# Filler matmuls, earlier zero stores and an early start of two w2 passes in a decode step with its gradients

## The chip, the core and the metric

The kernel runs on one core of one Trainium2 chip. The metric is device time in microseconds (us), median of several runs. "Span" is the time from the first to the last instruction of one profiled execution; all positions such as "at 341.5" are us from the start of that span. Engines: TensorE (PE; PEld are its weight loads), VectorE (DVE), ScalarE (ACT), GpSimd (POOL), SyncE (SP). SP and POOL issue nearly all transfers (DMA).

## What is computed

One token passes through two layers of type A (attention over a cache) and two of type B (a Mish MLP), in the order A, B, A, B, with the same weights for both A and for both B; then the gradients of everything are computed.

```python
def A(x, k_cache, v_cache, wq, wo):     # x: 1 x 1024, 32 heads of 128, 4 KV groups
    W = 4096                            # the last 4096 of 32768 cached positions
    q = x @ wq                          # wq: 1024 x 4096
    p = softmax(q k^T / sqrt(128));  o = p v
    return o @ wo                       # wo: 4096 x 1024
def B(x, w1, b1, w2):
    h = x @ w1 + b1                     # w1: 1024 x 3584
    return (h * tanh(softplus(h))) @ w2 # w2: 3584 x 1024
x = x + A(layernorm(x)); x = x + B(layernorm(x))
x = x + A(layernorm(x)); x = x + B(layernorm(x))
# outputs: x, and the gradients of x, k_cache, v_cache, wq, wo, w1, b1, w2 for a given grad_out
```

All arrays are bf16. The gradients of the two caches are 33.5 MB each and zero outside the last 4096 positions: the zeros have to be written all the same.

## The kernel before

**Stages.** The layers are called A1, B2, A3, B4 by their order. The program's order is: `attn_fwd` A1; `mlp_fwd` B2, which also reads w2 for the part of its backward that needs only the known last gradient; `attn_fwd` A3; `mlp_turn` B4, forward through w1 and backward through it in blocks of 512 columns; `attn_bwd` A3; the w2 pass of B4 (`w2_pass`); `mlp_bwd_w1` of B2; `attn_bwd` A1; at last the dW stage, which makes all weight gradients and the cache gradients as outer products, evicts them and stores them. Vectors are held as columns, 128 to a column; a matrix times a vector is a row of products of 128 x 128 blocks with the weight block as the stationary operand and the vector broadcast to 16 columns (`mv`, through `mm` at L222), or, where the rows are summed in four column groups of TensorE, with the vector stationary and 512 columns moving (`row_mm`).

**Order.** The schedule is manual: each engine executes its instructions in the order in which the Python code records them, and waits for others by semaphores. What stands ahead on an engine's queue is therefore done first. Weight tiles come through the pool `strm` of 6 buffers (NB): a load on SP waits until its buffer is free, and all that SP has behind it waits too. Transposes go to a PSUM pool of 4 buffers (`psum1`) and are evicted by ScalarE or VectorE (`evac`, L145 and L148). The work pool has one buffer for each tag; `scr`, `yr`, `rep8`, `de`, `db_row` and others share the tag "kp".

**Zeros.** 112 stores of a 0.5 MB tile of zeros `zt` fill the unused part of the cache gradients. `bg_zeros(n, after)` (L138) issues n of them on POOL once `after` is there; `zeros(n)` (L129) issues n on SP. The dictionary `Z` says how many at which place: A3d are issued within `attn_bwd` A3 after the wo loop, A1c at the start of `attn_bwd` A1 on POOL, A1d there after the wo loop, on SP. What is left over by then, 5 stores, is issued one at a time between groups of nine dW jobs (`zeros(1)`, L1145).

**attn_bwd.** wo has 16 tiles, nine of which are kept in SBUF; the last seven ("late") are read again. The gradient is broadcast to all partitions (`bcast_row`, tile `gbc`: a VectorE copy `rep8` L580 and 8 matmuls). Then come products with kept tiles (`bwd_rows2`), 32 row matmuls into `drow`, and a loop over the late tiles: T(i) transposes half a tile, has ScalarE evict it and VectorE multiply and sum the other half with `gbc` (L781); M(i) multiplies the transposed half and, between tiles, does pieces of other preparation (`fill` in A3, `nextprep` in A1). After it: dO to a row and back (`dps`, `qps`), `rows_mm` with V (tile `d`), the softmax gradient, `cols_mm` with K, 64 row matmuls with wq (`nrow`), their copy `yr` (`rows_copy`, L238), a selection (`rows_sel2`), and the gradient of the norm (`ln_bwd`). The last work of `prep` in A1 is `db1_out`, the small bias gradient with its POOL store, and `rows_put` of dq for the dW stage.

**w2 pass.** For each of 14 tiles: forward products, 8 transposes (L602), eviction by ScalarE (L603), a VectorE reduction with `gbc` (L605), and, one tile later, the backward products.

**dW stage.** Each chunk is four matmuls into PSUM, evictions by both engines into a staging slot of 0.5 MB, and a store on SP.

Of the kernel before, what the change touches and what calls it, by code (L numbers as in the profile page):

```python
# [8 lines left out]
FP32 = mybir.dt.float32  # L9
BF16 = mybir.dt.bfloat16  # L10
# [4 lines left out]
P = 128  # L15
# [8 lines left out]
def kernel(  # L24
# [117 lines left out]
    def evac(out_ap, in_ap, cd, ca, how=None):  # L142
# [3 lines left out]
        else:  # L146
            ev[1] += ca
            nc.scalar.copy(out_ap, in_ap)  # L148

    def shaped(t, shape):  # L150
        n = 1
        for k in shape[1:]:
            n *= k
        ap = t[0:shape[0], 0:n]
        if len(shape) == 3:
            return ap.rearrange("p (a b) -> p a b", a=shape[1])
        if len(shape) == 4:
            return ap.rearrange("p (a b c) -> p a b c", a=shape[1], b=shape[2])
        return ap
# [110 lines left out]
    def ln_fwd(x_col, name):  # L270
# [3 lines left out]
        sps = sm_tile(P, 2 * TD)  # L274
        nc.tensor.matmul(sps[:], lhsT=onesD[:], rhs=xx[:], start=True, stop=True)
        s12 = work.tile([P, 2], FP32, name="s12")
        nc.vector.reduce_sum(s12[:], sps[:].rearrange("p (a b) -> p a b", a=2), axis=AX.X)
# [13 lines left out]
    def ln_bwd(dn_ps, n32, rstd, g_col, name, nxt):  # L291
# [4 lines left out]
        sps = sm_tile(P, 2 * TD)  # L296
        nc.tensor.matmul(sps[:], lhsT=onesD[:], rhs=tt[:], start=True, stop=True)
        ab = work.tile([P, 2], FP32, name="ab")
        nc.vector.reduce_sum(ab[:], sps[:].rearrange("p (a b) -> p a b", a=2), axis=AX.X)
# [286 lines left out]

    def w2_pass(a_bf, g_bf, x_col, xname, wgname, gbc, zn):

        acc = wide(TD + NW2)
        wg = keep.tile([P, NW2, 2], FP32, name=wgname)  # L590
        held = []

        def bwd1(w, c):
            for dch in range(TD):
                mv(acc, TD + c, w[:, 1, dch * P:(dch + 1) * P], g_bf[:, dch:dch + 1], False, dch == TD - 1)

        for c in range(NW2):
            w = pre.pop(0) if pre else w2_load(c)
            fwd_rows2(acc, w, c, a_bf, c == 0, c == NW2 - 1)
            ps = psum1([P, 8, P], BF16, "tps")  # L600
            for b in range(TD):
                nc.tensor.transpose(ps[:, b, :], w[:, 1, b * P:(b + 1) * P], ident_bf[:])  # L602
            nc.scalar.copy(w[:, 1, :], ps[:].rearrange("p b c -> p (b c)"))  # L603
            scr = work.tile([P, D], BF16, name="scr", tag="kp")
            nc.vector.tensor_tensor_reduce(out=scr[:], in0=w[:, 0, :], in1=gbc[:], scale=1.0, scalar=0.0,  # L605
                                           op0=ALU.mult, op1=ALU.add, accum_out=wg[:, c, 0:1])
            if held:
                bwd1(held.pop(), c - 1)
            if c == NW2 - 2 and zn:
                bg_zeros(zn, wg[:, c, :])  # L610
            held.append(w)
        bwd1(held.pop(), NW2 - 1)
        x_new = keep.tile([P, TD], FP32, name=xname)
        nc.vector.tensor_add(x_new[:], x_col[:], acc.cols(0, TD))
        nc.vector.tensor_copy(wg[:, :, 1:2], acc.cols(TD, TD + NW2)[:, :, None])
        return x_new, wg

    def mlp_fwd(x_col, lname, g_bf):

        n32, n_bf, rstd = ln_fwd(x_col, lname)  # L620
        sv = dict(n32=n32, rstd=rstd)
        hacc = wide(TF)
        h_init(hacc.t, 0, TF)
        for i in range(2 * TD):
            t, hf = i // 2, i % 2
            w = w1_load(i)
            for b in range(NW2):
                fb = hf * NW2 + b
                o = (b // 2) * 2 * P + b % 2
                mv(hacc, fb, w[:, o:o + 2 * P - 1:2], n_bf[:, t:t + 1], False, t == TD - 1)  # L630
        a_bf = pair_col("a", lname, TF)
        dact = keep.tile([P, TF], FP32, name=f"dact_{lname}")
        gbc = bcast_row(g_bf)
        m = mish_exp(hacc.cols(0, TF), TF)
        mish_w(m, hacc.cols(0, TF))
        nc.vector.tensor_mul(a_bf, m["hr"], m["w_"])
        mish_y(m)
        nc.vector.tensor_mul(dact[:], m["y"], m["r"])
        sv["dact"] = dact
        x_new, wg = w2_pass(a_bf, g_bf, x_col, f"x_{lname}", "wg4", gbc, Z["B2"])  # L640
        return x_new, sv, wg
# [103 lines left out]
    def attn_bwd(g_col, g_bf, lname, sv, first, nxt):  # L745
# [9 lines left out]
        drow = sm_tile(P, 512)  # L755
        wdo = work.tile([P, NO - NR], FP32, name="wdo")
        bwd_rows2(dacc, wo_kept[NR - 1], NR - 1, g_bf, started=False)
        for dch in range(TD):
            for q in range(4):
                row_mm(drow, q, g_bf[:, dch:dch + 1], wo_rows[:, 4 * q:4 * q + 4, dch * P:(dch + 1) * P], dch == 0, dch == TD - 1)  # L760
# [13 lines left out]

        def T(i):
            c = late[i]
            if c not in held:
                held[c] = wo_load(c)
            w = held[c]
            xpose(*nat_blocks(w[:, 1, :]), "a")  # L780
            nc.vector.tensor_tensor_reduce(out=w[:, 0, :], in0=w[:, 0, :], in1=gbc[:], scale=1.0, scalar=0.0,  # L781
                                           op0=ALU.mult, op1=ALU.add, accum_out=wdo[:, i:i + 1])

        def M(i, _):
            c = late[i]
            w = held.pop(c)
            for dch in range(TD):
                mv(dacc, 2 * c + 1, w[:, 1, dch * P:(dch + 1) * P], g_bf[:, dch:dch + 1], False, dch == TD - 1)
            if i == 0:
                for j in range(4):  # L790
                    mm(dacc.cols(j, 16)[:, 0:13:4], de[:, j * P:(j + 1) * P], ident_bf[:, 0:P:32], False, True)
            if first and i in (1, 3, 5):
                fill(1, ["V", "K", "wq"], "a")
            if not first and i:
                nextprep()

        pipe(list(range(len(late))), T, M)
        if first:
# [12 lines left out]
        if first:  # L811
            fill(1, ["K", "wq"], "a")
        dps = psum1([HQ, P], BF16, "dps")
        nc.tensor.transpose(dps[:, 0:P], do_p[:].rearrange("p t c -> p (t c)"), ident_bf[:])
# [4 lines left out]
        if first:  # L819
            fill(1, ["K", "wq"], "a")  # L820
        qps = psum1([P, NO, 2], FP32, "qps")
        for e in range(2):
            mm(qps[:, :, e], drf[:, e * P:(e + 1) * P], fold16[:], e == 0, e == 1)
        sv["dorep"] = pad_cols(pad, qps[:].rearrange("p c e -> p (c e)"), 1.0, f"do_{lname}")
        top("halves")
# [4 lines left out]
        else:  # L830
# [9 lines left out]
            ])  # L840
            nextprep(2)
        scr = work.tile([P, WC], BF16, name="scr", tag="kp")
        sdp = work.tile([P, 2], FP32, name="sdp")
# [16 lines left out]
        if first:  # L860
            fill(100, ["K"], "a")
        else:
            nextprep(1)
        for hf in range(2):
            half_T(ds, dsT, hf, "va"[hf])
# [6 lines left out]
        if first:  # L872
            fill(100, ["wq"], "av")
        else:
            prep.append(lambda: rows_put(area["Rq"], 1, "dq", "heads"))
        nrow = acc_tile(512)
# [6 lines left out]
        nps = sm_tile(P, TD)  # L883
        rows_sel2(rows_copy(nrow, "v"), Cols8(nps, True))
        return ln_bwd(nps[:], sv["n32"], sv["rstd"], g_col, lname, nxt)


# [152 lines left out]
    def after_do():  # L1040
        s0, s1, tall["w2"], area["do3"], area["q3"], _, r1 = cut_up(wo_flat, 0, (1024, 1024, 2560, 512, 512, 512, 2048))
        area["spread"] = [s.rearrange("p (j x) -> p j x", x=P) for s in (s0, s1)]
# [20 lines left out]

    Z = dict(B2=3, A3=16, B4=[5, 2, 1, 2, 1, 2, 6], A3c=6, A3d=29, W1=3, A1c=6, A1d=25)

# [41 lines left out]
    x3, sA3 = attn_fwd(x2, "A3", False)  # L1107
    g3, g3b, sB4 = mlp_turn(x3, "B4", wg4, gcol, "A3")
    g2, g2b = attn_bwd(g3, g3b, "A3", sA3, True, "B2")
    x4, wg2 = w2_pass(sB4["a_bf"], g2b, x3, "x_B4", "wg2", bcast_row(g2b), 0)  # L1110
    dh_of(wg2, "B2", sB2)
# [4 lines left out]
    def db1_out():  # L1116
        db1 = work.tile([P, 2, NW2], BF16, name="db1")
        nc.vector.tensor_add(db1[:], sB4["dh"][:].rearrange("p (c t) -> p t c", t=2), sB2["dh"][:].rearrange("p (c t) -> p t c", t=2))
        db_row = work.tile([NW2, P, 2], BF16, name="db_row", tag="kp", padded_shape=[NW2, WC // 2, 2])
        for t in range(2):  # L1120
            dbps = psum1([NW2, P], BF16, "dbps")
            nc.tensor.transpose(dbps[:], db1[:, t, :], ident_bf[:])
            nc.vector.tensor_copy(db_row[:, :, t], dbps[:])
        nc.gpsimd.dma_start(out_7.rearrange("(c x) -> c x", x=2 * P), db_row[:].rearrange("c p t -> c (p t)"))

# [53 lines left out]
```

## Time and profile before

| | |
|---|---|
| Time, median of 8 runs | 458.13 us (455.94 to 461.3) |
| Profiled execution, its own time | 459.46 us |
| Its span | 457.5 us |
| Moved by DMA | 172.23 MB, of it 98.58 MB written to HBM |
| Busy: PE / DVE / ACT / POOL | 71% / 52% / 49% / 13% of the span |
| Zero stores: on POOL / on SP | 82 / 30 |
| Mean granted TensorE clock | 0.739 |
| Last eviction of the dW stage ends | about 435.6 us |

The page cuts the span in 40 slices of 11.44 us; a digit gives the busy share of an engine in tenths, and the last row the transfer rate. An answer by stretches gives the same for chosen windows: busy us and number of instructions in brackets for PE, PEld, DVE, ACT and POOL, then the granted clock of TensorE as a share, the busy share of the DMA engines and GB/s. The chain of waits lists, in order of time, the start, the length and what the end of the program was waiting for at that moment; "DMA w_c<-in_B_w_dram" is the time from issue to landing of a load. The stages by their places in this execution: `attn_bwd` A3 from about 191 to 246, the w2 pass of B4 to 269, `mlp_bwd_w1` to 298, `attn_bwd` A1 to 348, dW from then on.

### The profile page before, as it was taken

To read this page: it belongs to the slowest core of one execution; us is meant where nothing else is said; L and a number is where in the kernel's file an instruction comes from. 1 tells how busy PE (TensorE), PEld (TensorE's weight loads), DVE (VectorE), ACT (ScalarE), POOL (GpSimd) and SP (SyncE) were. 2 spreads that over 40 slices of the span, in tenths; PEclk is the share of its full clock that TensorE was granted. 3 is DMA by queue.
4 is the path that set the end of the run, shared out by engine and by line. 5 is a ranking of instruction groups with operands and counts; after the bars stand their busy time and mean duration, and the time that the engine had idled before them with its cause. 6 is when DMAs were issued, how large, how long until landed. Compare 5 with 4: busy or idle time off the path is not lost.

```text
span 457.5 us, 11888 instructions
## 1 busy us (share of the span) xinstructions
PE 324.2 (71%) x5080; PEld 221.1 (48%) x5080; DVE 236.7 (52%) x489; ACT 225.0 (49%) x262; POOL 59.8 (13%) x152
## 2 busy tenths in 40 slices
PE   0465755586897989868897887776856858888700
PEld 0243534485567979845885877753522111112100
DVE  3124101385423757653265853572326978999900
ACT  1122100165332858774582653435214988999900
POOL 2000000002422112421331020062010000000000
PEclk9999555577977989995798788979675555556555
DMA  8999999989999998999999998999993999999997
GB/s 315 388 413 422 408 408 356 405 285 342 417 415 374 404 338 288 404 410 418 415 414 388 323 360 315 341 385 401 415 368 121 406 415 401 415 414 407 420 415 307
DMA packets 52256, 172.23 MB, mean 376 GB/s; under 512 B 5200, under 2 KB 12396, under 8 KB 51180
## 3 DMA queue, kind: packets, MB, share of 16 engines
q1 hardware_dynamic: 40256, 128.47, 72.6%
q0 software_dynamic: 11904, 43.01, 23.4%
q8 instruction: 39, 0.64, 0.5%
q14 instruction: 13, 0.11, 0.1%
q10 hardware_dynamic: 44, 0.01, 0.0%
HBM read 72.89 MB, written 98.58 MB: 375 GB/s over the span
## 4 chain that ended last, share of the span: by engine, by line
PE 23%; ACT 13%; DMA 9%; issue 4%; DVE 3%; DVEq 0%; POOL 0%; ACTq 0%; SPq 0%; POOLq 0%
PE tps L186 7%; ACT wq_b L148 6%; PE ops L222 5%; DMA w_c<-in_B_w_dram 4%; PE acc L222 4%; DMA out_dram<-st_o 2%; PE sm L222 2%; ACT wo_b L148 2%; DMA wo_c<-in_A_wo_dram 2%; ACT st_o L148 2%; PE d L222 2%; PE tps L602 1%; ACT wo_c L148 1%; ACT V L148 1%; DMA out_dram<-db_row 1%
## 5 line engine op out<-in xcount | busy, mean ns | idle before, releaser
L138 POOL DMA_DIRECT2D out_dram<-zt x82 | 43.6, 535 | 46.3 <-DMA out_dram<-zt 43.5
L222 PEld LDWEIGHTS <-w_c 128*128 128x128 bf16 x1120 | 35.8, 101 | 20.8 <-DMA w_c<-in_B_w_dram 13.4
L603 ACT COPY w_c<-tps 128x1024 bf16<-128x1024 bf16 x28 | 28.3, 1012 | 24.0 <-PE tps L602 12.5
L222 PE MATMUL ops<-V 2*128 2x512 bf16 (+1 forms) x160 | 33.5, 579 | 6.5 <-ACT wq_b L148 3.5
L605 DVE CUSTOM_DVE_ANT_0 scr<-w_c,gbc 128x1024 bf16<-128x1024 bf16 x28 | 34.2, 1221 | 6.8 <-DMA w_c<-in_B_w_dram 4.9
L145 DVE CAST wq_b<-ops 128x1024 bf16<-128x1024 f32 (+1 forms) x31 | 33.8, 1147 | 3.8 <-PE ops L222 3.3
L148 ACT CAST wq_b<-ops 128x1024 bf16<-128x1024 f32 (+1 forms) x33 | 33.7, 1140 | 2.2 <-PE ops L222 2.0
L148 ACT COPY K<-tps 128x1024 bf16<-128x1024 bf16 x19 | 18.7, 1024 | 29.3 <-PE tps L186 29.3
L222 PE MATMUL ops<-wo_b 2*128 2x512 bf16 x120 | 23.3, 567 | 10.9 <-ACT wq_b L148 7.2
L222 PEld LDWEIGHTS <-V 128*128 128x128 bf16 (+2 forms) x416 | 14.0, 101 | 27.6 <-issue 27.3
L222 PE MATMUL q<-wq_b,nA_pair 128*32 128x512 bf16 x128 | 12.6, 473 | 16.7 <-DMA wq_b<-in_A_wq_dram 15.2
L781 DVE CUSTOM_DVE_ANT_0 wo_c<-wo_c,gbc 128x1024 bf16<-128x1024 bf16 x14 | 16.4, 1219 | 12.5 <-DMA wo_c<-in_A_wo_dram 5.3
L148 ACT COPY w_b<-tps 128x1024 bf16<-128x1024 bf16 x20 | 19.5, 1015 | 5.3 <-PE tps L186 4.9
L145 DVE COPY K<-tps 128x1024 bf16<-128x1024 bf16 x13 | 8.8, 689 | 24.9 <-DMA wq_b<-in_A_wq_dram 14.1
L602 PE MATMUL tps<-ident_bf,w_c 128*128 128x128 bf16 x224 | 21.5, 254 | 0.0
L186 PE MATMUL tps<-ident_bf,w_c 128*128 128x128 bf16 x224 | 17.7, 241 | 4.2 <-DMA w_c<-in_B_w_dram 4.2
L222 PEld LDWEIGHTS <-wo_b 2*128 2x128 bf16 (+1 forms) x152 | 5.7, 100 | 29.3 <-issue 28.7
L186 PE MATMUL tps<-ident_bf,K 128*128 128x128 bf16 x256 | 19.6, 234 | 0.1
L148 ACT COPY w_c<-tps 128x768 bf16<-128x768 bf16 (+1 forms) x14 | 11.6, 829 | 15.9 <-PE tps L186 15.9
L222 PE MATMUL acc<-a_pair,w_c 128*128 128x16 bf16 x448 | 15.8, 172 | 4.7 <-DMA w_c<-in_B_w_dram 3.7
L145 DVE COPY w_c<-tps 128x1024 bf16<-128x1024 bf16 (+1 forms) x18 | 11.7, 660 | 13.6 <-PE tps L186 9.6
L148 ACT CAST K<-ops 128x1024 bf16<-128x1024 f32 x18 | 17.5, 1014 | 2.5 <-PE ops L222 1.9
(321 smaller groups left out, 665.5 us busy)
## 6 DMA issues: line engine op xcount, KB each, us to landing
out_dram<-zt POOLq DMA_DIRECT2D x82, 512.0 KB, 10.4
out_dram<-zt SPq DMA_DIRECT2D x30, 512.0 KB, 7.9
wo_c<-in_A_wo_dram SPq DMA_DIRECT2D x28, 512.0 KB, 8.0
w_c<-in_B_w_dram SPq DMA_DIRECT2D x32, 448.0 KB, 6.3
w_c<-in_B_w_dram SPq DMA_DIRECT2D x28, 512.0 KB, 6.5
out_dram<-wq_b SPq DMA_DIRECT2D x17, 512.0 KB, 9.9
wq_b<-in_A_wq_dram SPq DMA_DIRECT2D x16, 512.0 KB, 10.8
out_dram<-K SPq DMA_DIRECT2D x8, 1024.0 KB, 8.6
```

The lines of the kernel that those rows point to most:

```text
L138: nc.gpsimd.dma_start(zero_jobs.pop(0), zt[:])
L145: nc.vector.tensor_copy(out_ap, in_ap)
L148: nc.scalar.copy(out_ap, in_ap)
L186: nc.tensor.transpose(ps[:, b, :], ap, ident_bf[:])
L222: nc.tensor.matmul(out_ap, lhsT=lhsT, rhs=rhs, start=start, stop=stop, skip_group_check=True, **kw)
L602: nc.tensor.transpose(ps[:, b, :], w[:, 1, b * P:(b + 1) * P], ident_bf[:])
L603: nc.scalar.copy(w[:, 1, :], ps[:].rearrange("p b c -> p (b c)"))
L605: nc.vector.tensor_tensor_reduce(out=scr[:], in0=w[:, 0, :], in1=gbc[:], scale=1.0, scalar=0.0, op0=ALU.mult, op1=ALU.add, accum_out=wg[:, ...
L781: nc.vector.tensor_tensor_reduce(out=w[:, 0, :], in0=w[:, 0, :], in1=gbc[:], scale=1.0, scalar=0.0, op0=ALU.mult, op1=ALU.add, accum_out=w ...
```

## The change

A function `warm(n)` is new: n matmuls of the identity with itself, 512 columns wide, into a PSUM tile that nobody reads. It is called with 6 in the norm of A3 forward, with 7 in the norm's gradient ahead of `attn_bwd` A1, and with 4, 2, 2, 3 and 3 within `attn_bwd` A1: 27 matmuls.

In `attn_bwd` T(0), T(1) and M(0) are issued before the row matmuls `drow`; the products with `de` move from M(0) to M(1).

The w2 pass becomes a class whose steps can be called apart. In B2 the broadcast is recorded ahead of the w1 loop, the transposes of tile 0 ahead of the second part of the Mish activation, and `mish_y` and `dact` after the last tile. In B4 tile 0 is transposed while `yr` is copied in `attn_bwd` A3 ("copy"), its forward products and eviction follow the selection ("sel"), and those of tiles 1 and 2 follow the norm gradient's sum ("ln").

`rows_put` of dq leaves the list `prep` and stands behind the copy of `yr`. `db_row` lies in a part of the kept wo area that was unused, not in a tile of tag "kp".

Zeros: A3d 29 to 26, A1c 6 to 3, A1d 25 to 36. The zeros of the dW stage become none.

```diff
+    def warm(n):
+        ps = psum1([P, 4, P], FP32, "wps")
+        for _ in range(n):
+            nc.tensor.matmul(ps, lhsT=ident_bf[:], rhs=ident_bf[:, None, :].to_broadcast([P, 4, P]),
+                             start=True, stop=True, skip_group_check=True)
...
@@ ln_fwd @@
+        if name == "A3":
+            warm(6)
...
@@ ln_bwd @@
+        if nxt == "A1":
+            warm(7)
+        if nxt == "B2":
+            hook("ln")
...
-    def w2_pass(a_bf, g_bf, x_col, xname, wgname, gbc, zn):
+    class W2Pass:
+        def tp(self, c):       # transposes of tile c
+        def fwd(self, c):      # forward products
+        def tc(self, c):       # eviction of the transposes (and tp, where not done)
+        def bwd(self, c, g_bf):
+        def rest(self, done, g_bf, x_col, xname, gbc, zn, last=None):
+            for c in range(NW2):
+                w = self.get(c)
+                if c >= done:
+                    self.fwd(c)
+                    self.tc(c)
+                scr = work.tile([P, D], BF16, name="scr", tag="kp")
+                nc.vector.tensor_tensor_reduce(out=scr[:], in0=w[:, 0, :], in1=gbc[:], ...)
+                if c:
+                    self.bwd(c - 1, g_bf)
...
@@ mlp_fwd @@
+        gbc = bcast_row(g_bf)
         for i in range(2 * TD):
...
-        gbc = bcast_row(g_bf)
         m = mish_exp(hacc.cols(0, TF), TF)
+        w2 = W2Pass(a_bf, "wg4")
+        w2.tp(0)
         mish_w(m, hacc.cols(0, TF))
         nc.vector.tensor_mul(a_bf, m["hr"], m["w_"])
-        mish_y(m)
-        nc.vector.tensor_mul(dact[:], m["y"], m["r"])
+        def last():
+            mish_y(m)
+            nc.vector.tensor_mul(dact[:], m["y"], m["r"])
...
@@ attn_bwd @@
+        T(0)
         bwd_rows2(dacc, wo_kept[NR - 1], NR - 1, g_bf, started=False)
+        T(1)
+        M(0)
         for dch in range(TD):
             for q in range(4):
                 row_mm(drow, q, ...)
...
-        pipe(list(range(len(late))), T, M)
+        for i in range(2, len(late) + 1):
+            if i < len(late):
+                T(i)
+            M(i - 1)
...
+        else:
+            warm(4)
         dps = psum1([HQ, P], BF16, "dps")
...
+        else:
+            warm(2)
         qps = psum1([P, NO, 2], FP32, "qps")
...
+        if not first:
+            warm(2)
         sv["dorep"] = pad_cols(pad, qps[:].rearrange("p c e -> p (c e)"), 1.0, f"do_{lname}")
...
             nextprep(2)
+            warm(3)
...
             nextprep(1)
+            warm(3)
         for hf in range(2):
             half_T(ds, dsT, hf, "va"[hf])
...
-        else:
-            prep.append(lambda: rows_put(area["Rq"], 1, "dq", "heads"))
...
-        rows_sel2(rows_copy(nrow, "v"), Cols8(nps, True))
+        yr = rows_copy(nrow, "v")
+        if first:
+            hook("copy")
+        else:
+            rows_put(area["Rq"], 1, "dq", "heads")
+        rows_sel2(yr, Cols8(nps, True))
+        if first:
+            hook("sel")
...
-    Z = dict(B2=3, A3=16, B4=[5, 2, 1, 2, 1, 2, 6], A3c=6, A3d=29, W1=3, A1c=6, A1d=25)
+    Z = dict(B2=3, A3=16, B4=[5, 2, 1, 2, 1, 2, 6], A3c=6, A3d=26, W1=3, A1c=3, A1d=36)
...
+    hooks.update(copy=lambda: w2p.tp(0), sel=lambda: w2_ahead([0]), ln=lambda: w2_ahead([1, 2]))
     g2, g2b = attn_bwd(g3, g3b, "A3", sA3, True, "B2")
-    x4, wg2 = w2_pass(sB4["a_bf"], g2b, x3, "x_B4", "wg2", bcast_row(g2b), 0)
+    x4, wg2 = w2p.rest(3, g2b, x3, "x_B4", bcast_row(g2b), 0)
...
-        db_row = work.tile([NW2, P, 2], BF16, name="db_row", tag="kp", padded_shape=[NW2, WC // 2, 2])
+        db_row = area["db"][0:NW2, 0:2 * P].rearrange("c (p t) -> c p t", t=2)
```

## Prediction

> **What bounds the kernel now.** I read the page's slices first. Each slice is 11.44 us; the rows that carry it:
>
> ```profile
> DVE  3124101385423757653265853572326978999900
> ACT  1122100165332858774582653435214988999900
> PEclk9999555577977989995798788979675555556555
> DMA  8999999989999998999999998999993999999997
> GB/s 315 388 413 422 408 408 356 405 285 342 417 415 374 404 338 288 404 410 418 415 414 388 323 360 315 341 385 401 415 368 121 406 415 401 415 414 407 420 415 307
> ```
>
> The transfers are the bound: 9 tenths or more nearly everywhere, at 400 to 420 GB/s. 172.23 MB (page, part 3) at 415 GB/s would take 415.0 us, so 42.5 of the 457.5 us are transfer time that isn't used. The change moves no bytes in or out of the total, so it can only win by filling dips. The deepest is slice 31 (121 GB/s); after it VectorE and ScalarE are full too, so it must be settled which of them sets the end. The stretches answer:
>
> ```profile
> core 0: us, PE busy (x) PEld busy (x) DVE busy (x) ACT busy (x) POOL busy (x), PEclk, DMA share, GB/s
> 330.00:340.00 10.00, 8.01 (x84) 3.04 (x84) 2.30 (x11) 1.70 (x3) 1.15 (x5) 0.75 1.03 417
> 340.00:342.00 2.00, 0.00 (x0) 0.00 (x0) 0.00 (x0) 0.52 (x1) 0.00 (x0) 0.98 0.76 309
> ...
> 344.00:346.00 2.00, 1.45 (x8) 1.39 (x8) 0.33 (x2) 0.00 (x0) 0.00 (x0) 0.50 0.00 0
> 346.00:348.00 2.00, 0.74 (x3) 0.51 (x3) 1.03 (x5) 0.00 (x0) 0.00 (x0) 0.50 0.03 8
> 348.00:350.00 2.00, 1.11 (x9) 0.28 (x9) 1.09 (x2) 0.93 (x2) 0.52 (x1) 0.50 0.01 1
> 350.00:352.00 2.00, 1.52 (x10) 0.34 (x10) 2.00 (x3) 2.00 (x4) 0.00 (x0) 0.50 0.39 162
> ...
> 434.00:444.00 10.00, 0.28 (x4) 0.00 (x0) 1.73 (x2) 1.45 (x2) 0.00 (x0) 0.50 1.03 416
> 444.00:454.00 10.00, 0.00 (x0) 0.00 (x0) 0.00 (x0) 0.00 (x0) 0.00 (x0) 0.50 1.02 410
> ```
>
> Two things are to be seen. From about 341.5 us (2.00 x 0.76 into its stretch) to 351.2 us (2.00 x 0.39 before the end of its) the transfer engines stand still: the zero stores of the last attention backward have run out and the first gradient isn't there yet. And the engines have evicted everything by about 435.6, while transfers go on at 410 GB/s until 454.6. So the dW stage is bound by its stores, by a margin of 19 us, and begins late. Last the chain of waits, three places of it:
>
> ```profile
> 198.28 7.99 DMA wo_c<-in_A_wo_dram
> 206.32 1.05 PE tps L186 x8
> ...
> 251.59 6.26 DMA w_c<-in_B_w_dram
> ...
> 337.77 4.91 DMA out_dram<-db_row
> 342.80 0.70 DVE yr L238
> ```
>
> 198.28: TensorE stands still for the seventh late wo tile. 251.59: the w2 pass waits for its own loads. 337.77: `yr` may not be written before the 7 KB bias gradient has left, because `db_row` (L1119) and `yr` (L236) share the one buffer of tag "kp", though TensorE finished the row matmuls at 339.8.
>
> **The sum that everything hangs on.** The stores of the dW stage run from 351.2 to 454.6, 103.4 us, then 2.9 us to the end of the span. One zero store is 0.524 MB; at 417 GB/s it is 1.257 us. Five of them lie in the dW stage: 6.3 us, so its own outputs take 97.1. Around the gap the change takes 3 zeros from the start of the last attention backward (A1c 6 to 3) and adds 11 to its end (A1d 25 to 36): 8 x 1.257 = 10.1 us more work for the queue, so the zeros last until 341.5 + 10.1 = 351.6. Before, the first store flowed at 351.2. So even if the chain of this stage isn't a microsecond shorter, the gap is closed (0 left), and the span is 351.6 + 97.1 + 2.9 = 451.6 less S, where S is by how much all earlier work arrives sooner. The zeros for this come from the dW stage (5) and from A3d (29 to 26), which is where S is earned or lost.
>
> **Part by part.**
>
> *Last attention backward (A1).* It decides only whether the first store is ready by 351.6 - S. In its favour: `db_row` in an own area ends the wait 339.8 to 342.80 (3.0 us) and TensorE's drop to half clock after it. The transposes T(0), T(1) and product M(0) now stand ahead of the 3.60 us of 32 row matmuls, so ScalarE evicts two tiles (2 x 1.02) under them: about 1.7 us. The tiles are there in time: VectorE took the first six without a stall from 300.19 on. Also SP's seventh load, issued at 306.33 when slot 0 came free, goes out at about 302; behind it on SP stand all the A1d zeros, which also start 4 us sooner. That is what lets three POOL zeros go (3.8 us of cover). The stretch 303 to 309 moved 382 GB/s and may gain 0.5 us by it. `rows_put` of dq moves directly behind the copy of `yr`: 4 POOL copies of 0.65 us in all, 8 transposes of 0.62, one eviction of 1.01, issued after POOL's bias store; POOL was through by 338.9, before `yr`, so 0. Its cover is the 0.70 us copy.
>
> The 21 fillers here cost TensorE time: no row shows them. Nearest is L222 `sm<-wo_b,gA_pair`, 512 columns in four column groups: 32 in 3.60 us at half clock, 1.91 at full, so 0.45 or 0.24 us for a full-width one. Together 9.5 or 5.0 us, placed where TensorE waits for vector work (1.98 us between 297.04 and 299.02, 1.25 before `dps`). The gain: `rows_mm` 3.36 at half clock to about 1.9. Net between -4 and +2 for the chain; I take a gain of 0 to 1. In sum the first store is ready about 5 us sooner, against a need of none beyond S: no price for the span.
>
> *Zeros in the dW stage.* Already counted. SP issues 36 zeros before the first store; it is held by them, one per 1.24 us as before, until the queue has room. Stores then start with evictions several us ahead; 31 slots lie before the first reuse, and at the end before, the backlog was 19 us or 15 stores.
>
> *The attention backward of A3.* M(0) ended at 198.06 to 198.2, which freed the slot of the seventh load. Now T(0), eviction (1.02), M(0) follow the broadcast that ended at 193.96: 0.46 + 1.02 + small waits + 0.37, so about 196. The load leaves 2.1 to 2.3 us sooner; its 7.99 us stay, as it shares the engines with POOL's zeros. TensorE stood 3.1 us at 206.32, so the loop in front, bound by evictions, leaves room for 2.2 to 2.9. I take 2.2. Bounds: 0 (the other evictions on ScalarE fill it), and 4 if TensorE, with less idling, keeps its clock over 205 to 215, where `d` took 3.60 instead of 1.9.
>
> *w2 pass of B4, opened ahead.* At `copy` 8 transposes (0.46) lie under the 0.70 copy of `yr`; at `sel` 16 products (0.37) under the copies of `tt` (0.36); at `ln` 32 products and 16 transposes, 1.7 us at full clock, in the 1.98 us until the broadcast, 3.3 at half clock. The clock was full there (240 to 246). What was exposed behind the broadcast, forward and transposes of tiles 0 and 1 ahead of the first backward product (247.55 to 250.4, SP's next load), falls to the 1.22 us of VectorE's first reduction: the load goes at about 248.5. Gain 2.0; bounds -1.3 (cold, late broadcast) and 3.1 (the whole pass at VectorE's pace, 14 x 1.27 from 247.15).
>
> *A3d 29 to 26.* Zeros ended at about 251, just when the loads began. They now end 3.8 us sooner, and the two items above bring the loads 4.2 sooner. Balance +0.4; if they bring only 1, transfers stand still for 2.8.
>
> *B2's w2 pass.* The broadcast goes ahead of the w1 loop, tile 0's transposes under the mish chain, and four small vector operations (0.8 us) behind the last reduction, where VectorE idled 1.27 us (to 110.67). TensorE's 0.9 us of transposes at half clock leave the head of the pass, VectorE's first reduction starts 0.7 sooner. Gain 0.7, bounds 0 and 1.
>
> *Six fillers in the norm of A3.* TensorE waited from 111.77 to 113.18 at half clock and got full clock only in the stretch 116 to 117. By the Trainium skill (TensorE: Matmul & The Clock Gate, Part 1: The HAM clock gate) the clock opens after some 3.4 us of sustained work in a free-running window, and the ramp is worth under 1% of a typical kernel: six fillers (2.7 us cold) then open nothing alone and delay q by 1.3, later partly regained: loss 0.5. By the row, if the clock opens one window sooner, q's 64 matmuls fall from 5.32 to 3.8: gain 1.1. I take 0, both ends kept.
>
> S = 0 + 0.7 + 2.2 + 2.0 = 4.9, and 0.5 from the denser stretch.
>
> **Rivals.**
>
> *Main.* 451.6 - 5.4 = 446.2 us of span, 11.3 less. The profiled execution took 459.46 with 457.5 of span; the median of the eight is 458.13. 458.13 - 11.3 = 446.8. S between 3 and 7 counts here: chance 0.64.
>
> *The work ahead doesn't pay, S 0 to 3.* For it: the loads share engines with zeros, and 48 instructions stand ahead of the broadcast. The three A3d zeros are then missed at 247 to 251. S about 1.5: 450.5. Chance 0.14.
>
> *More is set free, S over 7.* For it: half clock in 205 to 215 and 246 to 250. S about 8.5: 443.0. Chance 0.12.
>
> *Fillers exposed: slower.* TensorE runs in order, and each filler tile also takes one of four PSUM buffers, so it waits for the eviction four tiles back (up to 1.1 us). In A1: 21 x 0.45 + 6 x 1.1 = 16 us lost. The gap is then open again by what the chain loses against before beyond its gains; from 9 us net it brings no change, from 14 net a loss. All 16 exposed, nothing gained: 446.8 + 16 = 462.8. Against it: the waits they stand in are in the trace. No change by it (half exposed) 0.05, slower 0.05.
>
> About 0.5% (2.3 us) is what a measurement can tell from no change. Faster 0.90, same 0.05, slower 0.05. Range 442.5 to 451.5: S from 1 to 9.
>
> **What would show it.** Transfer share at 0.9 or more through the last attention backward up to the first store, no stretch near zero; `yr` no longer ended by the bias store; 36 zeros in a row on SP; the wait for the seventh wo tile begun near 196; the first w2 load about 1 us after the broadcast; evictions done some 20 us before the end. Wrong if a dip opens at the start of the w2 pass, or if transfers run dry before the first gradient store again.

## The result and the profile after

| | median | runs | ratio to before (95%) |
|---|---|---|---|
| before | 458.31 us | 32 (454.49 to 462.6) | |
| changed | 450.6 us | 11 (449.47 to 457.79) | 0.9844 (0.9814 to 0.9874) |

The medians are 7.7 us apart, where 11.3 were forecast. The ratio gives 7.1 us, with an interval of 5.8 to 8.5. The execution that was profiled first was disturbed (457.79 us), so what follows is the profile of a second run of the same kernel: 449.92 us with a span of 447.7, against the 459.46 and 457.5 of before. This pair is 9.5 us apart, some 2 more than the medians, so its numbers show where time goes, not to the microsecond how much.

The slices of the page, each 11.19 us now, and below them the stretches at the places that the forecast watched (us, then busy us of PE, PEld, DVE, ACT, POOL with instructions in brackets, granted TensorE clock, busy share of the transfer engines, GB/s):

```profile
DVE  3134201097332756683274854573259889999600
ACT  1121200075241867776593454545329899989600
PEclk9997555578876999999798788999785555555555
DMA  7999998999999998999999999999999999999994
GB/s 318 388 409 424 409 408 295 408 326 352 415 417 391 393 378 283 376 409 415 415 415 412 326 337 365 325 386 419 414 417 419 418 417 416 420 418 419 418 418 179
```

```profile
330.00:336.00 6.00, 3.16 (x29) 1.95 (x27) 2.96 (x10) 2.45 (x3) 0.52 (x1) 0.81 1.03 418
336.00:340.00 4.00, 3.03 (x18) 0.52 (x14) 4.00 (x4) 4.00 (x5) 0.00 (x0) 0.50 1.03 417
340.00:344.00 4.00, 3.17 (x18) 0.74 (x18) 4.00 (x5) 4.00 (x6) 0.00 (x0) 0.50 1.03 420
344.00:352.00 8.00, 6.29 (x30) 1.15 (x28) 7.66 (x8) 7.86 (x8) 0.00 (x0) 0.50 1.03 419
430.00:440.00 10.00, 0.00 (x0) 0.00 (x0) 0.00 (x0) 0.00 (x0) 0.00 (x0) 0.50 1.03 417
440.00:442.00 2.00, 0.00 (x0) 0.00 (x0) 0.00 (x0) 0.00 (x0) 0.00 (x0) 0.50 0.56 223
442.00:444.00 2.00, 0.00 (x0) 0.00 (x0) 0.00 (x0) 0.00 (x0) 0.00 (x0) 0.50 0.07 29
444.00:446.00 2.00, 0.00 (x0) 0.00 (x0) 0.00 (x0) 0.00 (x0) 0.00 (x0) 0.50 0.06 27
446.00:447.70 1.70, 0.00 (x0) 0.00 (x0) 0.00 (x0) 0.00 (x0) 0.00 (x0) 0.50 0.00 0
```

Two readings. The hole of slice 31 (121 GB/s before) is gone: from 330 to 440 the transfers are full without a break, and the dW stage is still bound by stores, as all evictions are done by about 421. And the last slice has fallen from 307 to 179 GB/s: after 440.4 us, the last moment at which at least 14 of 16 transfer engines had a packet under way, four microseconds pass at a share of 0.06 to 0.07. One engine of sixteen is 0.0625, and 417 GB/s by 16 is 26: a single transfer engine works off what it still has, and everything waits for it. Before, the same view showed no such phase:

```profile
452.00:454.00 2.00, 0.00 (x0) 0.00 (x0) 0.00 (x0) 0.00 (x0) 0.00 (x0) 0.50 1.02 408
454.00:456.00 2.00, 0.00 (x0) 0.00 (x0) 0.00 (x0) 0.00 (x0) 0.00 (x0) 0.50 0.31 123
456.00:457.50 1.50, 0.00 (x0) 0.00 (x0) 0.00 (x0) 0.00 (x0) 0.00 (x0) 0.50 0.01 5
```

Its last full moment was 454.3, 3.2 us before the end of the span; now it is 7.3 us before. The transfers are full for the last time 13.9 us sooner, and 4.1 of these are lost at the very end.

The chain of waits of the changed kernel, at the places that were shown of before, with the neighbours that matter (start, length, what was waited for):

```profile
194.14 0.62 PE gbc L229 x8
...
196.75 8.19 DMA wo_c<-in_A_wo_dram
...
242.61 0.91 PE gbc L229 x8
...
246.22 6.90 DMA w_c<-in_B_w_dram
...
256.40 5.50 DMA w_c<-in_B_w_dram
...
264.51 0.16 DVE x_B L657
...
329.13 0.53 POOL wo_b L986 x3
329.66 0.05 issue
329.70 0.62 PE rw L973 x8
330.32 0.86 PE sm L229 x8
```

196.75: the seventh wo tile is waited for from 2.6 us behind the start of the broadcast, and no longer from 4.9. 246.22 and 256.40: the chain now runs through two loads of the w2 pass, 12.4 us from issue to landing, where it ran through one of 6.26; TensorE itself stands still for loads for 4.4 us in this pass, before for 1.4. 329.13: `yr` is no longer held by the bias store, but the selection behind it is held by the moved `rows_put` of dq. Its four copies on POOL and eight transposes stand ahead of the selection on TensorE, 0.8 us in a place where nothing hung on them.

### The profile page after: what moved, and what is told of

Its sections match the earlier page's. It is cut to its first block, busy times and chain, and to the rows that moved or that the text cites. A ratio compares the mean times of both kernels' runs of the same rounds, so it can differ in the third digit from the quotient of the medians.

```text
span 455.6 us, 11941 instructions
## 1 busy us (share of the span) xinstructions
PE 331.3 (73%) x5107; PEld 226.6 (50%) x5107; DVE 236.7 (52%) x489; ACT 225.2 (49%) x262; POOL 56.5 (12%) x146
## 4 chain that ended last, share of the span: by engine, by line
PE 18%; DMA 12%; ACT 11%; issue 6%; DVE 3%; POOL 1%; DVEq 0%; SPq 0%; ACTq 0%; POOLq 0%
PE tps L193 6%; ACT wq_b L148 5%; DMA w_c<-in_B_w_dram 4%; PE ops L229 4%; DMA out_dram<-wo_b 3%; PE acc L229 3%; DMA out_dram<-st_o 2%; ACT wo_b L148 2%; DMA wo_c<-in_A_wo_dram 2%; ACT st_o L148 1%; PE d L229 1%; ACT wo_c L148 1%; ACT K L148 1%; PE sm L229 1%; PE wps L154 1%
## 5 line engine op out<-in xcount | busy, mean ns | idle before, releaser
L138 POOL DMA_DIRECT2D out_dram<-zt x76 | 40.4, 535 | 42.3 <-DMA out_dram<-zt 39.8
L229 PEld LDWEIGHTS <-w_c 128*128 128x128 bf16 x1120 | 37.6, 103 | 16.3 <-DMA w_c<-in_B_w_dram 13.0
L229 PE MATMUL ops<-V 2*128 2x512 bf16 (+1 forms) x160 | 34.7, 598 | 5.9 <-ACT wq_b L148 3.4
L229 PEld LDWEIGHTS <-V 128*128 128x128 bf16 (+2 forms) x416 | 14.2, 102 | 27.8 <-issue 27.6
L623 PE MATMUL tps<-ident_bf,w_c 128*128 128x128 bf16 x224 | 24.4, 277 | 0.7 <-DMA w_c<-in_B_w_dram 0.7
L229 PE MATMUL q<-wq_b,nA_pair 128*32 128x512 bf16 x128 | 10.9, 426 | 14.6 <-DMA wq_b<-in_A_wq_dram 14.5
L193 PE MATMUL tps<-ident_bf,K 128*128 128x128 bf16 x256 | 21.2, 246 | 0.0
L193 PEld LDWEIGHTS <-K 128*128 128x128 bf16 x256 | 17.9, 112 | 3.8 <-issue 3.7
L193 PE MATMUL tps<-ident_bf,w_c 128*128 128x128 bf16 x224 | 17.5, 239 | 2.8 <-DMA w_c<-in_B_w_dram 2.8
L623 PEld LDWEIGHTS <-w_c 128*128 128x128 bf16 x224 | 18.5, 124 | 1.3 <-DMA w_c<-in_B_w_dram 0.8
L193 PE MATMUL tps<-ident_bf,wq_b 128*128 128x128 bf16 x256 | 17.9, 237 | 1.4 <-issue 1.4
## 6 DMA issues: line engine op xcount, KB each, us to landing
out_dram<-zt POOLq DMA_DIRECT2D x76, 512.0 KB, 10.6
```

What stands on the lines that cost most here:

```text
L138: nc.gpsimd.dma_start(zero_jobs.pop(0), zt[:])
L193: nc.tensor.transpose(ps[:, b, :], ap, ident_bf[:])
L229: nc.tensor.matmul(out_ap, lhsT=lhsT, rhs=rhs, start=start, stop=stop, skip_group_check=True, **kw)
L623: nc.tensor.transpose(self.ps[c][:, b, :], w[:, 1, b * P:(b + 1) * P], ident_bf[:])
```

## What the experiments were to tell apart

Theory A: the time is the unused time of the transfers; the change wins because the stand-still ahead of the first gradient store is closed, and the moved zeros and the shorter chain are two ways to that same gain. Rival B: the fillers, or the faster chain by itself, make the gain. Theory C: the middle of the run gained what was forecast, and the end gave some of it back, since one transfer engine lags and no stand-still lets it catch up.

To compare the kernels I summed the unused transfer time from the transfer records (in steps of half a microsecond, one less the busy share of the 16 engines), cut at A1's broadcast, the first gradient store, the last moment of 14 busy engines, and the end of the span. It is one execution each; the time is the median of all. Shares a little under 1 count as well, so a long stage can have a few tenths without any break. What a higher rate at full share brings isn't in it.

| kernel | ahead of A1's broadcast | to the first store | dW | tail | sum | median us | ratio (95%) |
|---|---|---|---|---|---|---|---|
| before | 13.1 | 8.5 | 1.1 | 2.8 | 25.4 | 459.02 and 457.46 | |
| changed | 11.1 | 0.0 | 0.0 | 6.2 | 17.4 | 452.1 | 0.9842 (0.979 to 0.9894) |
| b5z | 9.1 | 2.0 | 3.2 | 2.8 | 17.1 | 453.11 | 0.9864 (0.9812 to 0.9916) |
| nofill | 12.4 | 0.2 | 0.0 | 6.1 | 18.8 | 453.88 | 0.9879 (0.9822 to 0.9935) |
| oldz | 10.6 | 0.2 | 0.0 | 4.9 | 15.8 | 449.88 | 0.9809 (0.9768 to 0.9849) |
| gbcback | 8.1 | 0.0 | 0.0 | 6.7 | 14.9 | 449.33 | 0.9819 (0.9769 to 0.9868) |
| dbonly | 8.4 | 3.7 | 1.1 | 2.8 | 16.0 | 454.45 | 0.9929 (0.9888 to 0.9969) |
| ordonly | 10.6 | 9.3 | 1.1 | 2.8 | 23.9 | 457.06 | 0.999 (0.9954 to 1.0026) |
| tail15 | 11.2 | 0.3 | 0.0 | 5.6 | 17.2 | 451.58 | 0.9862 (0.9808 to 0.9917) |

The second column says how much chance there is in one execution: `b5z` and `dbonly` have the code of before up to A1's attention backward, and still lie 4 to 5 us under it there. The other columns vary far less and fall into two kinds: kernels that keep a break ahead of dW and have a tail of 2.8, and kernels with no break and a tail of 4.9 to 6.7.

A second reading of the same traces shows how the tail comes about. Every store leaves sixteen completion records; the distance from the first to the last of them says how far its slowest share is behind the fastest. In us, for the store that begins to complete nearest to the time in the head:

| kernel | 332 | 353 | 391 | 418 | last store |
|---|---|---|---|---|---|
| before (break of 9.7 at 341.5) | 2.6 | 0.2 | 1.8 | 1.8 | 1.4 |
| ordonly (break) | 2.1 | 0.2 | 1.4 | 1.6 | 1.5 |
| dbonly (break of about 4) | 2.2 | 0.2 | 1.5 | 1.8 | 1.4 |
| b5z (break of about 3, and one of some 2 at 385) | 3.0 | 0.2 | 0.2 | 1.8 | 1.3 |
| changed | 2.8 | 3.9 | 5.2 | 6.0 | 6.2 |
| nofill | 2.8 | 3.4 | 4.5 | 5.4 | 6.0 |
| oldz | 2.5 | 3.3 | 3.8 | 4.2 | 3.8 |
| gbcback | 3.3 | 4.4 | 5.7 | 6.4 | 6.6 |
| tail15 | 3.3 | 4.3 | 4.6 | 5.4 | 5.4 |

At 332, ahead of the dW stage, all nine are alike, 2.1 to 3.3 us. A break brings the sixteen together again, to 0.2 us; without one the slowest keeps what it has lost and loses more. This is the mechanism of theory C, seen and not only inferred.

## The experiments

**The changed kernel once more (again).**

> The changed kernel once more, for an undisturbed trace and its own times beside the other three. Theory A (the stand-still of 9.7 us ahead of the first gradient store is closed, and little else is gained): 450.6 us, transfer share at 0.9 or more from 304 us to the end of the zeros. Theory B (the chain of the last attention backward is faster through the fillers, and this makes the gain): the same time. Theory C (the gain in the middle was as large as forecast, 5 us, and 3 us are lost again at the very end, because one transfer engine that fell behind no longer has a stand-still in which to catch up): the same time, with 5 us or more between the last full transfer slice and the end of the span, against 2.9 before.

Measured 452.1 us, 0.9842. This is the run shown above.

**Only the five zeros (b5z).** The kernel before, with the dW stage's zeros issued in A1:

```diff
-    Z = dict(..., A1c=6, A1d=25)
+    Z = dict(..., A1c=6, A1d=30)
```

> The kernel before with one number changed: A1d 25 to 30, so that no zero store is left for the dW stage. A: five stores of 1.257 us go into a stand-still of 9.7 us, so 6.3 us less, ratio 0.986, about 452 us. B: nothing of the chain is changed, so 0 to 1 us less. C: as A, less the part that a lagging engine gives back at the end, 4 to 6 us less.

453.11 us, 5.9 below its before. The stretches 336:344 and 344:352:

```profile
336.00:344.00 8.00, 2.84 (x16) 2.37 (x14) 1.13 (x4) 1.01 (x1) 0.00 (x0) 0.65 1.03 419
344.00:352.00 8.00, 4.73 (x27) 1.08 (x28) 6.69 (x11) 5.62 (x7) 0.52 (x1) 0.50 0.62 249
```

A break of about 3 us is left (0.38 of 8): five stores of 1.257 us fill 6.3 of the 9.7, and moving them is worth what the sum said for them. A second break, from 385 to 387, opens within the dW stage (shares of 0.08 and 0.13), so the small tail of this kernel isn't the work of the first break alone. This one number in `Z` has the larger part of the whole gain.

**Without fillers (nofill).** The changed kernel, with `warm` doing nothing:

```diff
     def warm(n):
+        return
```

> The changed kernel without its 27 filler matmuls. A: the chain of the last attention backward has some 5 us of slack, so its time is that of the changed kernel within 1 us, 450 to 451.5. B: the half clock comes back in that chain, 3 to 5 us more, 454 to 455. C: as A.

453.88 us, 1.8 above the changed kernel on the same chip, with intervals that overlap widely. That misses what A expected (450 to 451.5) and is next to what B did (454 to 455). In the profile the fillers do what they are for: the products with V (tile `d`, both attention backwards, ns min/median/max) of the changed kernel, and then without fillers:

```profile
L229 PE MATMUL d<-V,do_pad x64: 379/379/391, 209.7 to 312.0; 128*32 128x512 bf16 x64
```

```profile
L230 PE MATMUL d<-V,do_pad x64: 504/634/634, 210.3 to 316.6; 128*32 128x512 bf16 x64
```

In A1 the 32 take 1.91 us instead of 3.6, and the gradient's copy `yr` starts 36.2 us behind the broadcast instead of 38.7. Neither matters: without fillers the first store is issued at 341.9, in time for zeros that last as long (0.2 us unused). B in its full form fails, since 5.1 of the 6.9 us are still there without fillers; their own share is 0 to 2 us, and these runs don't settle it.

**Zeros where they were (oldz).** The changed code with the old numbers:

```diff
-    Z = dict(..., A3c=6, A3d=26, W1=3, A1c=3, A1d=36)
+    Z = dict(..., A3c=6, A3d=29, W1=3, A1c=6, A1d=25)
```

> The changed kernel with the zero numbers of before (A3d 29, A1c 6, A1d 25, five zeros left in the dW stage). A: the shorter chain alone closes 8 of the 9.7 us of stand-still, and three more zeros fill the dip at the start of the w2 pass; so the zeros are worth no more than 2 us on top of the chain: 449.5 to 452.5. B: as the changed kernel, 450.6, since the chain is the same. If on the other hand the zeros are what matters and not the chain: 456 to 457.

449.88 us, 0.9809: not slower than the changed kernel, rather faster. The first store goes out at 337.4, while the last zeros of A1 are still in flight, and five zeros fill in between dW jobs as before. No break is left:

```profile
336.00:344.00 8.00, 6.12 (x32) 1.23 (x28) 7.92 (x7) 7.97 (x9) 0.10 (x1) 0.50 1.03 418
344.00:352.00 8.00, 6.46 (x32) 1.28 (x30) 7.89 (x8) 7.86 (x9) 0.00 (x0) 0.50 1.03 415
```

So with the shorter chain the moved zeros are worth nothing; without it, five of them are worth 6 us. This is theory A.

**The broadcast of B2 back behind the w1 loop (gbcback).**

```diff
-        gbc = bcast_row(g_bf)
         for i in range(2 * TD):
...
+        gbc = bcast_row(g_bf)
         m = mish_exp(hacc.cols(0, TF), TF)
```

> The changed kernel with one part undone: in B2 the broadcast of the gradient stands behind the w1 loop again. In the trace of the changed kernel its 0.69 us copy and 1.03 us of matmuls stand ahead of the first w1 products on TensorE's queue, and the first freed buffer's load leaves at 72.49, not at 70.94; the stretch 72 to 80 moved 297 GB/s, before 373. Theory A2 (this dip is what B2's gain was lost to): 1.5 us less than the changed kernel, 449, and the dip gone. Rival (the dip is made good within B2, which waits for other loads anyway): the same time.

449.33 us. The stretch 72 to 80 in the changed kernel and in this one:

```profile
72.00:80.00 8.00, 4.30 (x140) 3.94 (x139) 0.00 (x0) 0.00 (x0) 0.00 (x0) 0.50 0.83 299
```

```profile
72.00:80.00 8.00, 3.94 (x105) 3.23 (x101) 0.00 (x0) 0.00 (x0) 0.00 (x0) 0.50 1.02 375
```

The dip comes from the broadcast: its copy `rep` and its 8 products (1.03 us at half clock) stand ahead of the first w1 products, so that the first freed w1 buffer is refilled at 72.49 us and not at 70.94, as before, and all loads behind it are 1.55 us later. The dip is shown to be the broadcast's; that undoing it gains 1 us is likely, but within the intervals.

**Only the place of db_row (dbonly).** The kernel before, with `db_row` in its own part of the kept wo area:

```diff
-        db_row = work.tile([NW2, P, 2], BF16, name="db_row", tag="kp", padded_shape=[NW2, WC // 2, 2])
+        db_row = area["db"][0:NW2, 0:2 * P].rearrange("c (p t) -> c p t", t=2)
```

> The kernel before with one part of the change: the bias gradient's row lies in an own area, so that the copy of the row sums no longer waits for its store. Theory A (what ends the stand-still of 9.7 us is how early the first gradient store is ready; chain and zeros are two ways to the same gain): the wait of 3.0 us and the half clock behind it go, 3 to 4 us less, 454.5 to 455.5. Rival (the wait only moves to what stands behind it on the queues): 0 to 1 us less.

454.45 us over 12 runs, 3.0 below its before. `yr` starts 39.5 us behind A1's broadcast instead of 43.8, at once when the row matmuls end. The stretches:

```profile
336.00:344.00 8.00, 4.51 (x26) 1.39 (x26) 5.81 (x12) 4.29 (x5) 0.52 (x1) 0.50 0.47 187
344.00:352.00 8.00, 6.54 (x36) 1.47 (x32) 8.00 (x8) 7.85 (x10) 0.00 (x0) 0.50 1.02 409
```

About 4 us of the stand-still remain (this execution, at 450.12 us, was its fastest).

**Only the order of transposes and products (ordonly).** The kernel before, with T(0), T(1), M(0) ahead of the row matmuls:

```diff
+        T(0)
         bwd_rows2(dacc, wo_kept[NR - 1], NR - 1, g_bf, started=False)
+        T(1)
+        M(0)
         for dch in range(TD):
...
-            if i == 0:
+            if i == 1:
                 for j in range(4):
...
-        pipe(list(range(len(late))), T, M)
+        for i in range(2, len(late) + 1):
+            if i < len(late):
+                T(i)
+            M(i - 1)
```

> The kernel before with one part of the change: T(0), T(1) and M(0) ahead of the row matmuls in both attention backwards. A: 2.2 us in A3, 1.7 us in A1, and the seventh load with the zeros behind it 4 us earlier, which closes no more of the stand-still than the chain does: 3 to 4.5 us less, 454 to 455.5. Rival (ScalarE's evictions bound both loops, so that nothing is gained at their ends): within 1 us of before.

457.06 us over 12 runs, 0.999: nothing. The stand-still is untouched:

```profile
336.00:344.00 8.00, 3.17 (x32) 2.26 (x33) 1.21 (x4) 1.01 (x1) 1.15 (x5) 0.77 0.52 213
344.00:352.00 8.00, 4.56 (x24) 1.76 (x25) 5.29 (x12) 3.77 (x5) 0.52 (x1) 0.50 0.21 85
```

In A3 the transposes that waited for the seventh tile start 1.6 us sooner (11.4 us behind the broadcast instead of 13.0), but in A1 the last ones come 1.0 later (14.2 instead of 13.2).

**Lighter load on the last transfer engine (tail15).** The changed kernel, with the first four zeros of each call on SP cut in two, 120 and 8 partitions:

```diff
-        for _ in range(min(n, len(zero_jobs))):
-            nc.sync.dma_start(zero_jobs.pop(0), zt[:])
+        for k in range(min(n, len(zero_jobs))):
+            dst = zero_jobs.pop(0)
+            if k < 4:
+                nc.sync.dma_start(dst[0:120], zt[0:120, :])
+                nc.sync.dma_start(dst[120:128], zt[120:128, :])
+            else:
+                nc.sync.dma_start(dst, zt[:])
```

> The changed kernel with four of the zero stores on SP cut in two, 120 and 8 partitions; by the Trainium skill (DMA: Bandwidth & Descriptors, the section on why a DMA increments its semaphore by 16) such a store goes to 15 and to 8 engines and leaves the last one out, while the bytes stay the same. In the trace of the changed kernel one transfer engine works alone for the last 4 to 5 us, at 27 GB/s: some 130 KB, four shares of 32 KB. Theory C with the last engine as the one that lags: 3 to 4 us less, 447, and 3 us instead of 7.2 between the last full stretch and the end. If another engine lags: no change, or up to 0.5 us more. If the time at the end is no engine's lag but a latency of the last stores: no change and the same picture.

451.58 us and still 6.3 us from the last full moment to the end of the span. The lag grows here as in the others, 3.3 us at 332 and 5.4 at the end. The tail didn't go, so either the lagging engine isn't the one that this spares, or the cut doesn't spare it; the records don't name the engine. Which one it is, and why it lags, stays open.

Not tried: the five zeros and `db_row` together without the rest (alone they gave 3.0 and 5.9 us; together they would close the stand-still and get the longer tail, 9.6 less 2 to 4, which is an estimate of 451 to 453), `oldz` and `gbcback` together, and the w2 pass and the order each taken out of the changed kernel.

## Why the forecast was right, and why its gain was 3.6 us too large

**The gap is closed without the chain being shorter: right.** All five kernels with the changed code have 0.0 to 0.3 us unused between A1's broadcast and the first store, where it was 8.5, and nothing in dW, where it was 1.1. That is 9.6 us, against 9.7 in the forecast. The zeros run in a row on SP from 295.7 to 338.1, and the first store, whose group of products started at 333.9, goes out behind them at 339.5. So the zeros and not the chain now set it, as the sum said.

**"Then 2.9 us to the end of the span": here it failed.** The tail was taken over unchanged. The first table shows 2.8 unused in all four kernels that keep a break ahead of dW (about 4 us are enough, `dbonly`), and 4.9 to 6.7 in all five that have none; in this pair 3.4 more. That a single engine is busy in those 4 us is shown by the share, and that a break lets it catch up by the completion records: 0.2 us behind after the break of before, 3.9 at the same place without one. The break of 9.7 us that the sum closed was thus not all loss, and the 2.9 us were no constant. After the break the lag also grows less (by 1.2 us from 353 to the last store, by 2.2 in the changed kernel); why is open. A little is given back, which the forecast didn't have either: the last 104.7 us up to the last full moment move 43.8 MB, 418 GB/s, where before the stage moved 42.4 MB in 103.0 us (its 1.1 unused taken off), 412. On 104 us that is 1.6; what raises the rate is not shown.

**S: not found.** The forecast had earlier work arrive 5.4 us sooner, of which 3.8 pay for the three zeros taken from A3d, so 1.6 of unused time were to go ahead of A1's broadcast. The pair shows 13.1 to 11.1; but the old code alone varies from 8.4 to 13.1, and the changed code with the early broadcast from 10.6 to 12.4. A gain of 1.6 can't be told from none. A1's broadcast does start 6.3 us sooner in the pair (292.7 for 299.0), but 1.8 MB fewer have been moved by then, which is 4.3 us of zeros put off. Of its terms:

- *Attention backward of A3, 2.2.* The mechanism was right and the size too: the seventh load leaves 2.61 us behind the broadcast instead of 4.94, and `yr` starts 43.6 behind it instead of 48.5. Half of these 4.9 is clock: with the products with V as slow as before (`nofill`, 3.5 us) it is 46.1, a gain of 2.4, and the old code with them fast (`b5z`, 1.9 us) has 46.3. It pays only through the zeros, for the transfers had no unused time at all in this stage, 0.0 before and after. The clock there isn't in the hands of the code: the granted clock of 208 to 216 was 0.52 before and 0.95 in `b5z`, with the same instructions up to there.
- *w2 pass opened ahead, 2.0.* The first load leaves 2.45 us behind the broadcast's start instead of 3.90, 1.45 sooner. The end of the pass comes after 22.0 instead of 22.3, so 0.3 are left. In the other profiles of the changed code it is between a gain of 1.1 and a loss of 3.9, the loss in `oldz`, where all 29 zeros of A3d are still under way beside the loads. The 4.4 us for which TensorE stands waiting for loads, before 1.4, say why: the pass is bound by its loads, and work ahead of a load that comes no sooner is turned into waiting for it.
- *B2, 0.7.* The four vector operations behind the last reduction and the transposes do gain (88 to 112 moves 343 GB/s, before 316), but the broadcast's new place, costed at nothing, takes 1.55 us from the loads in front. `x` of B2 comes at 110.6, before at 110.7: 0, in a spread of 109.4 to 110.8 among the four kernels with the old code of B2. The working looked at what the broadcast leaves and not at what it now stands ahead of.
- *Six fillers in the norm of A3, 0.* In four profiles with the fillers the products with wq start 2.9 to 3.6 us behind `x` of B2, where it was 2.5, and the last of them starts at 6.9 to 7.8; before at 7.4, without fillers at 7.8. They begin later and run faster, as both bounds had it, and 0 stands. The granted clock, which changes at distances of 3.4 us or a multiple of it here, goes to full 3.8 to 5.6 us behind `x` with the fillers, 6.0 before and 6.7 without them.

The sum, then: 11.3 forecast, less 3.4 for the tail, plus 1.6 for the rate, less the 1.6 ahead that can't be found, is 7.9; 7.7 were measured. The tail is its largest term. That it meets so closely is luck in part: the terms are of one pair of executions, which has 2.0 us less unused time ahead and is 9.8 us apart in span.

**A1's chain, "about 5 us sooner": more, and of no use.** From the broadcast to the first dW products it took 49.4 us before and 41.2 now. `db_row` was put at 3.0 and gave 5.1 alone; the order was put at 1.7 and gave nothing alone (-0.7); the fillers, put at 0 to 1, gave 2.7 (43.9 without them). All of it beyond the need went into a store waiting behind zeros. As the only edit, `db_row` is worth 3.0 us, since then the stand-still is still there to be filled.

**The rival of fillers exposed** is ruled out: without them the kernel isn't faster. **The rival of work ahead that doesn't pay** (450.5) has the time that was measured, and half of its reason, since S can't be found; but its mark, transfers missing at the start of the w2 pass, is absent (the stretch 240 to 248 has a share of 1.01 and 390 GB/s), and the larger loss lies in the tail, which it didn't name. (By the forecast's own sum an S of 1.5 is 450.7 and one of 8.5 is 443.7, not 450.5 and 443.0; nothing hangs on it.)

## What to carry to other kernels

When transfers bound the whole run, sum their unused time by stage before and after: a chain that ends 5 us sooner under full transfers is worth nothing, and two edits that fill the same hole are not added: five moved zeros gave 5.9 us alone and nothing beside the shorter chain (`oldz`). Ask of every moved instruction what it now stands ahead of, and of every hole that is closed what it did for others, since the tail of the run may have leaned on it. A fixed "end of the span" belongs in the range of a forecast and not among its constants.

## What the runs showed of the hardware

The sixteen transfer engines don't finish a row of stores together. After 100 us of stores without a break the slowest was about 4 us behind the next (0.42 MB were left after the last full moment, before 0.14 MB), and a break of about 4 us ahead of the stage (`dbonly`) was enough for the tail to stay at 3.1. In the changed kernel the distance between the first and the last completion of a store grows from 2.8 us at 332 to 6.2 at 440. Two steps of 0.6 in it, for the stores that end at 350.2 and 441.7, follow instruction loads of 8 KB at 348.2 and 440.4; the rest is steady growth, and its cause is open.

The Trainium skill (DMA: Bandwidth & Descriptors, section Latency and other measured facts) says that two of the engines are usually slower in traces and guesses at the descriptor rings of GpSimd's queue. No run here shows which engine it is. The guess finds no support: from 339.0 us on GpSimd's queue moved nothing more in the changed kernel, and the distance still grew from 3.1 to 6.2; and with six more zeros on GpSimd (`oldz`, 82 for 76) the tail was not longer but shorter, 4.9 for 6.2.
